# A fused RWKV-6 attention and multiplicative FFN kernel: GpSimd's data arithmetic moved to other engines, k by DMA transpose from unit 7 on, a new order of work

## The chip, the cores and the metric

The kernel runs on one core of a Trainium2 chip. A core has engines that run their own instruction queues in order: TensorE (PE in the profile, its weight loads PEld), VectorE (DVE), ScalarE (ACT), GpSimd (POOL) and SyncE (SP, which only issues DMAs here). They wait for each other by semaphores. The metric is the device time of one execution in microseconds (us), lower is better. Before the change it is 173.02 us, the median of 3 runs (172.81 to 173.9).

## The reference, cut to what matters

```python
# r, k, v, w: [4 batches, 8 heads, 768 steps, 48], u: [8, 48]
state = np.zeros((B, H, D, D))
for t in range(S):
    cur = np.einsum('bhd,bhe->bhde', u[None] * kt, vt)
    y[:, :, t] = np.einsum('bhd,bhde->bhe', rt, state + cur)
    state = wt[:, :, :, None] * state + np.einsum('bhd,bhe->bhde', kt, vt)
x = y.transpose(0, 2, 1, 3).reshape(B * S, H * D)      # [3072, 384]
out = ((x @ w1) * (x @ w2)) @ w3 @ w_out               # d_ff 1024
```

All inputs and the output are float32 in memory.

## The kernel before, in words

Time is cut into 6 chunks of 128 steps. A **unit** is one chunk of two batches (units 0 and 1 are one batch each), 13 units in all, unit t at `UNITS[t]`. Within a chunk the recurrence is written as masked matmuls; between chunks a state of 48 x 48 per head is carried.

For unit t the steps are, by their names in the program (a name is followed by the unit, and by the batch or group):

- loads: `win`, `kin`, `rin`, `vin`. k, r and v are cast to bf16 on the way, which is done on GpSimd's DMA queue; w stays float32.
- decay: `ln` (ScalarE, log of w), `cs` (TensorE, running sum over time by a triangular matrix), `pc`, `ne`, `e`, `iw` (ScalarE, exponentials of it).
- scaled operands: `KRk` (VectorE, k times a decay), `rw` and `KRr` (VectorE, r times decays). Units 0 to 2 (`RAW`) do r in transposed form with `csT` and `et` instead.
- transposes: `trr` and `trk` on TensorE into PSUM with `trre` and `trke` copying to SBUF, or `dtr` and `dtk` as DMA transposes on SP's queue. Before, `dtr` and `dtk` serve units 9 to 12.
- the u term: `rk` (r times k), `ruk` (times u), `dg` (sum over a head), `dv` (v times that sum).
- scores: `m` (TensorE), then either `msk` (VectorE, product with the mask straight from PSUM) or, for the pairs in `POOL_MASK`, `mcp` (ScalarE, PSUM to SBUF) and `maff` (GpSimd, an affine select in place).
- output: `y` (TensorE: scores times v plus r times state), `yb` (VectorE, adds dv; for units in `Y_PE` TensorE adds dv with an identity, `yd`, and `yb` is a plain copy), then a transpose into xT: `yt` and `xT`, or two DMA transposes `dty`, one for each batch (units 8 to 12).
- state: `kv` (TensorE), `T` (VectorE, sum with the old state), `S` (times the chunk's decay), `Sb` (bf16 copy).

The FFN folds w3 and w_out into one matrix w34 at the start: `wt` (transposes on TensorE), `w3Te`, `wm` (64 matmuls), `w34e`. Then **block** t does for four groups of 256 hidden units (two groups of 512 for units 0 and 1) `a` and `b` (TensorE, x times w1 and w2), `asb` (copy of a to SBUF), `abT` (VectorE, the product), and for each batch `o` (TensorE, times w34), `osb` (copy) and `st` (store). `a` and `b` need xT, `o` needs all of w34.

The order of everything is written out by hand. `ORDER` lists every step once with the engine or queue that issues it (`abT_3_1@DVE`), and each engine runs its own steps in that order. `PLACES` gives each step's buffer or PSUM banks. `warm7@15` is 15 filler matmuls into bank 7, which keep TensorE busy while it has nothing else. The lists are data only: the code in `unit`, `block`, `w34_block` and `loads` registers one function for each name, and the last loop of the kernel calls them in the order given.

Lines of the profile that matter here: L389 the unit loads, L400 to L415 the weight loads, L486 and L491 `cs`, L575 `trr`, L590 `trk`, L579 and L594 the copies behind them, L569 and L584 `dtr` and `dtk`, L598 `rk`, L618 `ruk`, L624 `dg`, L633 `dv`, L647 `m`, L653 `mcp`, L661 `maff`, L666 `msk`, L700 `yd`, L706 and L709 `yb`, L718 `dty`, L728 `yt`, L732 `xT`, L752 `T`, L757 to L761 `S`, L786 `a` and `b`, L792 `asb`, L796 `abT`, L802 `o`, L808 `osb`, L813 `st`, L373 the fillers.

Of the kernel before, what the change touches and what calls it, by code (L numbers as in the profile page):

```python
# [862 lines left out]
```

## Time and profile before

| | before |
|---|---|
| median of 3 runs | 173.02 us |
| span of the profiled execution | 172.3 us |
| busy: TensorE / VectorE / ScalarE / GpSimd | 160.0 / 133.2 / 94.1 / 97.8 us |
| fillers on TensorE (L373) | 27, 9.9 us |
| GpSimd: dv (9), maff (8), S (8) | 12.0, 8.8, 7.7 us |
| GpSimd's wait before maff, for mcp | 29.0 us |
| median time of a two-batch k load from issue to landing | 9.3 us |

How to read the profile: busy is the time in which an engine has an instruction running, with overlaps counted once; an instruction's own duration is a little more than its distance to the next one of a row, since instructions overlap at their ends. A busy TensorE is not a TensorE at its peak, since the ends of matmuls are modelled. Spans on GpSimd are rough. The part of the kernel that bounds it is read from the stretches in which an engine stands still, and from the chain of work that ended last. Issuing a load costs GpSimd 1.13 to 1.16 us each, which counts as its busy time.

### The profile page before, as it was taken

The numbers are of one execution on the slowest core, as the hardware profiler recorded it, in microseconds if no ns is written. First come the engines' busy times: TensorE is split into PE (matmuls) and PEld (weight loads), VectorE is DVE, ScalarE is ACT, GpSimd is POOL, SyncE is SP. The second block draws the span as 40 slices with busy tenths as digits, with TensorE's granted clock in tenths as the row PEclk, the third lists the DMA queues.
The fourth block names the chain that finished last, engine by engine and source line by source line (L and its number), as shares of the span: only waits on it lengthen the run. The fifth ranks groups of instructions, "written<-read, shape, count | busy, mean of one in ns | idle before, by whom it ended". The sixth has DMA issues, their size and how long they took to land.

```text
span 172.3 us, 4685 instructions
## 1 busy us (share of the span) xinstructions
PE 160.0 (93%) x1956; PEld 119.6 (69%) x1956; DVE 133.2 (77%) x222; ACT 94.1 (55%) x161; POOL 97.8 (57%) x99
## 2 busy tenths in 40 slices
PE   5889999989999999599999999989989899999990
PEld 2364658558897789357778878667767687886750
DVE  4022798989889999969999899997988745856660
ACT  2125387867568699449888769855661430110301
POOL 7975968699988879694599972040057520000000
PEclk9999999999999999969999999999999999999999
DMA  4999999999999999999999999547879803400333
GB/s 70 159 200 171 235 178 189 177 184 163 170 196 175 163 161 197 175 160 205 71 61 234 119 68 157 111 125 158 166 154 111 142 12 83 137 0 4 137 137 139
DMA packets 98663, 24.36 MB, mean 141 GB/s; under 512 B 88833, under 2 KB 97026, under 8 KB 98642
## 3 DMA queue, kind: packets, MB, share of 16 engines
q0 software_dynamic: 81536, 16.06, 107.9%
q1 hardware_dynamic: 17106, 8.00, 18.9%
q8 instruction: 15, 0.25, 0.6%
q14 instruction: 6, 0.05, 0.1%
HBM read 27.79 MB, written 4.72 MB: 189 GB/s over the span
## 4 chain that ended last, share of the span: by engine, by line
PE 54%; DMA 17%; DVE 13%; ACT 5%; POOL 3%; issue 2%; SPq 2%; ACTq 0%; DVEq 0%; POOLq 0%
PE banks L786 25%; PE banks L802 13%; DMA xT<-yb 6%; DMA wo_bf<-in_moe_w_out_dram 6%; DMA win<-in_w_dram 5%; PE banks L437 4%; DVE abT L796 4%; DVE ruk L618 3%; PE banks L647 2%; PE banks L690 2%; PE banks L486 1%; SPq L813 1%; PE banks L744 1%; POOL w_bf L415 1%; DVE rk L598 1%
## 5 line engine op out<-in xcount | busy, mean ns | idle before, releaser
L786 PE MATMUL banks<-xT,w_bf 128*128 128x256 bf16 (+1 forms) x624 | 70.3, 265 | 1.9 <-DMA xT<-yb 1.9
L786 PEld LDWEIGHTS <-w_bf 128*128 128x128 bf16 x624 | 55.9, 98 | 10.4 <-issue 1.9
L796 DVE TENSOR_TENSOR abT<-a_sb,banks 128x512 bf16<-128x512 f32 x48 | 32.1, 680 | 8.8 <-PE banks L786 8.1
L792 ACT COPY a_sb<-banks 128x512 f32<-128x512 f32 x38 | 22.2, 593 | 27.6 <-DVE abT L796 16.0
L802 PE MATMUL banks<-w,abT 128*128 128x384 bf16 x192 | 36.0, 334 | 0.0
L661 POOL TENSOR_SCALAR_AFFINE_SELECT Mbf<-Mbf 128x1024 bf16<-128x1024 bf16 x8 | 8.8, 1096 | 31.5 <-ACT Mbf L653 29.0
L802 PEld LDWEIGHTS <-abT 128*128 128x128 bf16 x192 | 18.3, 99 | 11.2 <-issue 1.0
L666 DVE TENSOR_TENSOR Mbf<-banks,mask 128x1024 bf16<-128x1024 f32 x16 | 19.3, 1216 | 2.3 <-PE banks L647 2.1
L808 ACT COPY osb<-banks 128x384 f32<-128x384 f32 x18 | 8.7, 491 | 20.7 <-PE banks L802 12.4
L389 POOL DMA_DIRECT2D kin<-in_k_dram x13 | 14.6, 1128 | 1.9 <-DVE KK L505 1.2
L389 POOL DMA_DIRECT2D vin<-in_v_dram x13 | 14.8, 1136 | 0.8 <-DMA wo_bf<-in_moe_w_out_dram 0.7
L389 POOL DMA_DIRECT2D rin<-in_r_dram x13 | 14.7, 1135 | 0.2 <-issue 0.2
L389 POOL DMA_DIRECT2D win<-in_w_dram x12 | 13.9, 1156 | 1.5 <-DMA wo_bf<-in_moe_w_out_dram 1.2
L633 POOL TENSOR_TENSOR dv<-vin,dg 128x768 bf16<-128x768 bf16 (+1 forms) x9 | 12.0, 1345 | 4.4 <-DMA vin<-in_v_dram 1.6
L470 ACT ACTIVATE lw<-win 128x768 bf16<-128x768 f32 (+1 forms) x13 | 10.4, 806 | 7.1 <-DMA win<-in_w_dram 7.1
L709 DVE TENSOR_TENSOR yb<-banks,dv 128x768 bf16<-128x768 f32 x10 | 9.5, 954 | 3.8 <-issue 1.7
L437 PE MATMUL banks<-wo_bf,w3T 128*128 128x384 bf16 x64 | 11.9, 326 | 0.3 <-DMA wo_bf<-in_moe_w_out_dram 0.3
L373 PE MATMUL banks<-zeros 128*128 128x512 bf16 x27 | 9.9, 508 | 1.8 <-DVE zeros L288 1.8
L624 DVE TENSOR_REDUCE dg<-ruk 128x16 f32<-128x768 bf16 (+1 forms) x13 | 11.4, 879 | 0.1
L500 ACT ACTIVATE NEt<-banks 128x768 bf16<-128x768 f32 (+1 forms) x13 | 10.0, 778 | 1.5 <-PE banks L491 0.9
L647 PE MATMUL banks<-RT,KT 64*128 64x128 bf16 x192 | 8.7, 218 | 1.9 <-DVE RT L579 1.4
L653 ACT CAST Mbf<-banks 128x1024 bf16<-128x1024 f32 x8 | 8.2, 1020 | 3.9 <-PE banks L647 2.7
(86 smaller groups left out, 232.7 us busy)
## 6 DMA issues: line engine op xcount, KB each, us to landing
out_dram<-osb SPq DMA_DIRECT2D x24, 192.0 KB, 2.1
win<-in_w_dram POOLq DMA_DIRECT2D x11, 384.0 KB, 8.9
kin<-in_k_dram POOLq DMA_DIRECT2D x11, 192.0 KB, 9.3
rin<-in_r_dram POOLq DMA_DIRECT2D x11, 192.0 KB, 9.4
vin<-in_v_dram POOLq DMA_DIRECT2D x11, 192.0 KB, 7.6
w_bf<-in_moe_w_dram POOLq DMA_DIRECT2D x8, 192.0 KB, 7.1
w_bf<-in_moe_w_dram POOLq DMA_DIRECT2D x4, 256.0 KB, 8.5
w_bf<-in_moe_w_dram POOLq DMA_DIRECT2D x2, 512.0 KB, 8.8
```

Of the source, the lines that this page charges most:

```text
L389: QUEUE[eng].dma_start(dst, src)
L437: nc.tensor.matmul(one(f"wm{fi}")[:, :DM], lhsT=x[:, gi, :], rhs=wo_bf[:, gi, :], start=(gi == 0), stop=(gi == FI - 1))
L470: nc.scalar.activation(LW[:, :, :D], ww, Act.Ln)
L500: nc.scalar.activation(dst, cs_view(), Act.Exp, scale=-1.0)
L624: nc.vector.reduce_sum(dgs, ruks, axis=AX.X)
L633: e.tensor_mul(dvs, vv, dgs[:, :, None].to_broadcast([C, bh, D]))
L647: nc.tensor.matmul(o[:, e, q, :], lhsT=KTs[a:a + PAD, b * HP + q, :], rhs=RTs[a:a + PAD, b * HP + q, :], start=True, stop=True)
L666: nc.vector.tensor_mul(Mbf[m].rearrange("s j q t -> s (j q) t"), mview().rearrange("s j q t -> s (j q) t"), mask[:, None, :].to_broadcast( ...
L786: nc.tensor.matmul(o[:, f, :], lhsT=wt[:, di, fi * P:(fi + 1) * P], rhs=x[:, di, :T], start=(di == 0), stop=(di == DI - 1))
L792: copier(eng)(sa, one(f"a{t}_{g}"))
L796: nc.vector.tensor_mul(ab[:, g * per:(g + 1) * per, :T], sa.rearrange("p (f t) -> p f t", t=T), one(f"b{t}_{g}").rearrange("p (f t) -> p f ...
L802: nc.tensor.matmul(one(f"o{t}_{b}")[:, :DM], lhsT=ab[:, fi, b * C:(b + 1) * C], rhs=w34[:, fi, :], start=(fi == 0), stop=(fi == FI - 1))
```

## The change

Five things change. The code that computes stays the same but for a few places; most of the difference is in the two lists.

1. **GpSimd does no arithmetic on data.** All 13 `dv` and all 11 `S` run on VectorE (before 4 and 3). `maff` runs on VectorE as a product with the mask, in place in SBUF. GpSimd keeps the loads, LT, I128 and the mask, and two affine selects on a small u matrix. `POOL_MASK` now names 12 pairs instead of 8, so 12 of the 24 masks go by `mcp` and `maff`, and 12 by `msk` (before 16).
2. **k by DMA transpose from unit 7** (the eighth): `dtk_7` and `dtk_8` are new, and `dty_7_0`, `dty_7_1` too. `trr` stays on TensorE for units 7 and 8.
3. **The last tile in halves:** o_12_0, osb_12_0 and st_12_0 become two parts of 192 columns.
4. Unit 11's `dg` is computed on TensorE (`PE_DIAG`): a DMA transpose of rk (`dtd_11`), six matmuls of 8 columns (`d_11`), a copy (`dcp_11`), with a small matrix of u made by `ucol`, `ublk` and `ublk2`. `yd` serves units 5 and 7 instead of 0, 1 and 2.
5. **A new order, new banks and buffers.** Among others win_0 goes to GpSimd's queue, eight of the stores to ScalarE's, the first block matmul is a_0_0 instead of a_2_0, and some `asb`, `osb`, `trre`, `trke`, `w3Te`, `yb`, `xT` and `Sb` change between ScalarE and VectorE.

Steps by engine, before and after, where the number changes:

| step | engine | before | after |
|---|---|---|---|
| dv | VectorE / GpSimd | 4 / 9 | 13 / 0 |
| S | VectorE / GpSimd | 3 / 8 | 11 / 0 |
| maff | VectorE / GpSimd | 0 / 8 | 12 / 0 |
| msk | VectorE | 16 | 12 |
| mcp | ScalarE | 8 | 12 |
| asb | ScalarE / VectorE | 38 / 10 | 42 / 6 |
| osb | ScalarE / VectorE | 18 / 6 | 20 / 5 |
| trre | ScalarE / VectorE | 3 / 3 | 6 / 0 |
| st | SP / ScalarE | 24 / 0 | 17 / 8 |
| trk, yt, yd | TensorE | 9, 8, 3 | 7, 7, 2 |
| DMA transposes | SP | 18 | 23 |
| fillers | TensorE | 27 | 29 |

The core of the diff; of the two lists only the pieces that the prediction speaks of (the start up to the first block matmul, the stretch around unit 7, the end):

```diff
 RAW = {0, 1, 2}
 DMA_R = {9, 10, 11, 12}
-DMA_K = {9, 10, 11, 12}
-DMA_Y = {8, 9, 10, 11, 12}
-PE_DIAG = set()
-POOL_MASK = {(5, 1), (6, 1), (7, 1), (8, 1), (9, 1), (10, 1), (11, 1), (12, 1)}
-Y_PE = {0, 1, 2}
+DMA_K = {7, 8, 9, 10, 11, 12}
+DMA_Y = {7, 8, 9, 10, 11, 12}
+PE_DIAG = {11}
+HALF = {(12, 0)}
+POOL_MASK = {(0, 0), (3, 0), (5, 1), (6, 0), (6, 1), (8, 0), (8, 1), (9, 1), (10, 0), (10, 1), (11, 1), (12, 1)}
+Y_PE = {5, 7}
...
 ORDER = """
-urow@SP table@ACT padr_0@DVE padrr1@DVE padkk0@DVE win_0@SP padet0@DVE w3_1@POOL padkk1@DVE zeros@DVE ones2@DVE
-win_1@POOL padlw1@DVE padrr0@DVE padlw0@DVE ones@DVE padet1@DVE padr_1@DVE w3_5@POOL w3_3@POOL wo_0@POOL rin_1@POOL
-wo_1@POOL LT@POOL rin_0@POOL kin_1@POOL ln_1@ACT ln_0@ACT kin_0@POOL warm7@15 cs_0@PE I128@POOL warm7@3 wt_2_0@PE
-wt_6_0@PE wt_7_0@PE w3_0@POOL csT_0@PE wt_6_1@PE wt_7_1@PE w3Te_6_1@DVE wt_2_1@PE w3Te_7_1@DVE wt_3_0@PE w3_2@POOL
-w3Te_6_0@ACT csT_1@PE w3Te_2_1@DVE wt_3_1@PE w3Te_7_0@ACT w3Te_2_0@DVE cs_1@PE w3Te_3_1@DVE et_0@ACT w3Te_3_0@DVE
-et_1@ACT warm1@3 wm_3_0@PE win_2@POOL ne_1@ACT ne_0@ACT wm_6_0@PE ucast@ACT w3_4@POOL wm_7_0@PE warm1@1 wm_7_1@PE
-vin_0@POOL wm_2_0@PE w34e_7@DVE vin_1@POOL wm_2_1@PE KRk_1@DVE kin_2@POOL umm@PE KRk_0@DVE trr_1@PE trr_0@PE ucp@ACT
-KRr_1@DVE wm_6_1@PE pc_0@ACT w34e_2@ACT rk_1@DVE rin_2@POOL ruk_1@DVE wt_0_0@PE trk_0@PE rk_0@DVE wt_1_0@PE ruk_0@DVE
-trk_1@PE w34e_6@DVE wm_3_1@PE win_3@POOL trke_1@ACT KRr_0@DVE wt_1_1@PE trke_0@ACT wt_0_1@PE w3Te_1_0@DVE m_1_0@PE
-mask@POOL w3Te_0_0@ACT dg_0@DVE vin_2@POOL wm_1_0@PE w3Te_0_1@ACT msk_1_0@DVE wm_0_0@PE ln_2@ACT rin_3@POOL wm_0_1@PE
-dg_1@DVE w3Te_1_1@ACT pc_1@ACT m_0_0@PE w34e_3@ACT w34e_0@DVE cs_2@PE msk_0_0@DVE wm_1_1@PE ne_2@ACT wt_5_0@PE
-wt_5_1@PE kv_0@PE w3Te_5_0@ACT dv_0@POOL wt_4_0@PE S_0@DVE wt_4_1@PE w3Te_5_1@ACT w34e_1@DVE kv_1@PE csT_2@PE
-dv_1@POOL Sb_0@DVE S_1@DVE y_0@PE yd_0@PE pc_2@ACT w3Te_4_0@DVE y_1@PE win_4@POOL yd_1@PE yb_0@ACT padr_2@DVE
-KRk_2@DVE wm_5_0@PE et_2@ACT w3Te_4_1@DVE trk_2@PE kin_3@POOL trke_2@ACT rk_2@DVE trr_2@PE wm_4_0@PE ruk_2@DVE
-w1_0@POOL KRr_2@DVE wm_5_1@PE w1_1@POOL dg_2@DVE m_2_1@PE w34e_5@ACT wm_4_1@PE yb_1@ACT msk_2_1@DVE ln_3@ACT m_2_0@PE
-kv_2@PE dv_2@POOL iw_3@ACT msk_2_0@DVE cs_3@PE yt_0@PE w34e_4@ACT ne_3@ACT xT_0@DVE warm0@1 y_2@PE w2_0@POOL S_2@DVE
-yd_2@PE yt_1@PE w2_1@POOL yb_2@DVE ln_4@ACT vin_3@POOL rw_3@DVE warm1@3 yt_2@PE e_3@ACT cs_4@PE w1_2@POOL KRk_3@DVE
-xT_2@ACT KRr_3@DVE warm1@1 trk_3@PE w1_3@POOL pc_3@ACT xT_1@DVE trr_3@PE trke_3@ACT rk_3@DVE rin_4@POOL a_2_0@PE
-trre_3@DVE a_0_0@PE ruk_3@DVE asb_2_0@ACT w2_3@POOL ne_4@ACT dg_3@DVE m_3_1@PE a_2_1@PE w2_2@POOL Sb_1@ACT msk_3_1@DVE
...
-o_12_0@PE osb_12_1@DVE st_10_1@SP st_12_1@SP osb_12_0@ACT st_12_0@SP
+rin_0@POOL padet0@DVE padet1@DVE zeros@DVE ones2@DVE padkk1@DVE urow@SP ucast@ACT ones@DVE warm0@2 umm@PE table@ACT
+kin_0@POOL ucp@ACT padr_1@DVE padlw0@DVE win_0@POOL I128@POOL ln_0@ACT padr_0@DVE padkk0@DVE padlw1@DVE rk_0@DVE
+win_1@POOL w3_1@POOL LT@POOL warm0@4 trr_0@PE warm0@4 cs_0@PE ln_1@ACT csT_1@PE vin_1@POOL w3_3@POOL kin_1@POOL
+rin_1@POOL w3_5@POOL wo_0@POOL vin_0@POOL wo_1@POOL win_2@POOL cs_1@PE csT_0@PE wt_3_0@PE ne_1@ACT et_0@ACT KRr_0@DVE
+w3Te_3_0@DVE warm0@7 wt_2_1@PE ucol@SP ne_0@ACT KRk_1@DVE KRk_0@DVE warm1@4 trk_0@PE wt_2_0@PE kv_1@PE wt_3_1@PE
+rk_1@DVE padrr0@DVE ublk@DVE ruk_1@DVE w3Te_3_1@DVE mask@POOL w3_4@POOL kin_2@POOL rin_2@POOL w3_0@POOL win_3@POOL
+w3_2@POOL w3Te_2_0@ACT et_1@ACT pc_0@ACT w3Te_2_1@DVE padr_2@DVE pc_1@ACT S_1@DVE warm3@6 wt_6_1@PE wt_7_1@PE trr_1@PE
+trke_0@DVE m_0_0@PE trk_1@PE dg_1@DVE w3Te_7_1@ACT wt_7_0@PE ruk_0@DVE mcp_0_0@ACT trke_1@DVE dv_1@DVE KRr_1@DVE
+w3Te_7_0@DVE wm_2_0@PE kv_0@PE S_0@DVE dg_0@DVE wt_6_0@PE Sb_0@ACT w3Te_6_1@ACT m_1_0@PE wm_3_0@PE msk_1_0@DVE
+w3Te_6_0@DVE wm_2_1@PE wm_3_1@PE w34e_3@ACT ln_2@ACT wm_6_0@PE wm_6_1@PE w34e_6@DVE w34e_2@DVE y_1@PE cs_2@PE warm0@2
+wm_7_0@PE ne_2@ACT padrr1@DVE yb_1@DVE dv_0@DVE vin_2@POOL w1_1@POOL w2_1@POOL w1_0@POOL rin_3@POOL wt_5_1@PE
+wt_4_0@PE csT_2@PE wt_5_0@PE yt_1@PE w3Te_5_0@DVE xT_1@DVE KRk_2@DVE wm_7_1@PE w34e_7@DVE w3Te_5_1@DVE et_2@ACT
+w3Te_4_0@ACT pc_2@ACT maff_0_0@DVE rk_2@DVE ruk_2@DVE kin_3@POOL wm_5_0@PE trk_2@PE trr_2@PE wt_4_1@PE w3Te_4_1@ACT
+KRr_2@DVE wt_0_0@PE trke_2@ACT wm_5_1@PE wt_1_0@PE y_0@PE wm_4_0@PE wm_4_1@PE w3Te_1_0@ACT ln_3@ACT w34e_4@ACT
+yb_0@DVE w3Te_0_0@DVE w34e_5@DVE dg_2@DVE w2_0@POOL w2_3@POOL w1_3@POOL w1_2@POOL win_4@POOL w2_2@POOL m_2_1@PE
+yt_0@PE msk_2_1@DVE wt_1_1@PE wt_0_1@PE m_2_0@PE msk_2_0@DVE wm_0_0@PE cs_3@PE w3Te_0_1@ACT e_3@ACT w3Te_1_1@ACT
+Sb_1@ACT dv_2@DVE wm_0_1@PE y_2@PE yb_2@DVE wm_1_0@PE wm_1_1@PE yt_2@PE iw_3@ACT ne_3@ACT pc_3@ACT xT_2@ACT xT_0@DVE
+kv_2@PE S_2@DVE rw_3@DVE KRr_3@DVE a_0_0@PE a_2_0@PE w34e_0@ACT asb_0_0@ACT vin_3@POOL asb_2_0@DVE KRk_3@DVE rk_3@DVE
...
+KRr_8@DVE KRk_8@DVE dtk_7@SP trre_7@ACT abT_5_3@DVE dtk_8@SP st_3_0@ACT st_2_1@ACT b_6_3@PE trr_8@PE kv_7@PE rk_8@DVE
+a_6_3@PE kv_8@PE abT_5_2@DVE kin_11@POOL T_7@DVE T_8@DVE abT_5_1@DVE a_6_0@PE trre_8@ACT asb_6_3@ACT a_6_1@PE ln_9@ACT
+asb_6_1@ACT asb_6_0@ACT abT_6_3@DVE b_6_1@PE b_6_0@PE abT_6_1@DVE iw_9@ACT asb_5_0@ACT b_5_0@PE m_7_1@PE vin_12@POOL
+ublk2@POOL vin_10@POOL rin_9@POOL win_12@POOL abT_6_0@DVE m_8_1@PE a_6_2@PE msk_7_1@DVE asb_6_2@DVE abT_5_0@DVE
+dv_7@DVE mcp_8_1@ACT Sb_5@ACT o_4_0@PE osb_4_0@ACT cs_9@PE pc_9@ACT ln_10@ACT ne_9@ACT iw_10@ACT e_9@ACT m_7_0@PE
+b_6_2@PE o_4_1@PE msk_7_0@DVE abT_6_2@DVE maff_8_1@DVE S_7@DVE KRk_9@DVE m_8_0@PE o_5_0@PE y_7@PE cs_10@PE mcp_8_0@ACT
+ruk_8@DVE kin_12@POOL rin_10@POOL rin_11@POOL vin_11@POOL yd_7@PE maff_8_0@DVE o_6_1@PE yb_7@ACT Sb_7@ACT e_10@ACT
+ne_10@ACT pc_10@ACT osb_4_1@ACT o_6_0@PE kv_9@PE dty_7_0@SP dty_7_1@SP dg_8@DVE rw_9@DVE rk_9@DVE dv_8@DVE KRr_9@DVE
+T_9@DVE rw_10@DVE y_8@PE yb_8@DVE ruk_9@DVE ln_11@ACT st_3_1@ACT ln_12@ACT iw_11@ACT st_2_0@SP osb_6_0@ACT o_5_1@PE
+dtr_9@SP KRk_10@DVE rk_10@DVE dty_8_1@SP dtk_9@SP a_7_1@PE a_7_0@PE asb_7_0@ACT a_7_2@PE a_7_3@PE b_7_1@PE asb_7_2@ACT
...
+asb_12_3@DVE abT_12_2@DVE st_10_0@SP asb_12_1@ACT asb_12_0@ACT abT_12_1@DVE abT_12_0@DVE o_11_1@PE b_12_3@PE o_11_0@PE
+abT_12_3@DVE o_12_1@PE osb_11_1@DVE osb_11_0@ACT st_11_0@SP st_9_1@SP st_11_1@ACT o_12_0_1@PE osb_12_1@DVE o_12_0_0@PE
+st_12_1@SP osb_12_0_1@DVE st_12_0_1@SP osb_12_0_0@ACT st_12_0_0@SP
 """
...
     Et = many(N_ET, [C, BH, D], BF, "Et")
     NEt = many(N_NE, [C, BH, D], BF, "NEt")
     ETt = many(N_ETT, [P, NB * HP, C + 2], BF, "ETt")
-    RTr = many(N_RTR, [P, NB * HP, C], BF, "RTr")
+    RTr = many(N_RTR if RAW & DMA_R else 0, [P, NB * HP, C], BF, "RTr")
     KK = many(N_KK, [C, BH, PAD], BF, "KK")
     RR = many(N_RR, [C, BH, PAD], BF, "RR")
-    rkT = many(N_RKT, [P, NB * DI, C], BF, "rkT")
+    rkT = many(N_RKT if PE_DIAG else 0, [P, NB * DI, C], BF, "rkT")
     KT = many(N_KT, [P, NB * HP, C], BF, "KT")
     RT = many(N_RT, [P, NB * HP, C], BF, "RT")
     Mbf = many(N_M, [C, 2, HP, C], BF, "Mbf")
...
             def _(eng):
                 if c == 0:
                     nc.vector.tensor_mul(Sp, kvv(), PCb)
-                elif c < NC - 2:
-                    nc.gpsimd.tensor_mul(Sp, Tp, PCb)
                 else:
-                    nc.gpsimd.tensor_mul(Bp, Tp, PCb)
+                    e = nc.gpsimd if eng == "POOL" else nc.vector
+                    e.tensor_mul(Sp if c < NC - 2 else Bp, Tp, PCb)
 
             if c < NC - 2:
                 @op(f"Sb_{t}")
...
                 nc.vector.tensor_mul(ab[:, g * per:(g + 1) * per, :T], sa.rearrange("p (f t) -> p f t", t=T),
                                      one(f"b{t}_{g}").rearrange("p (f t) -> p f t", t=T))
         for b in range(nb):
-            @op(f"o_{t}_{b}")
-            def _(eng, b=b):
-                for fi in range(FI):
-                    nc.tensor.matmul(one(f"o{t}_{b}")[:, :DM], lhsT=ab[:, fi, b * C:(b + 1) * C], rhs=w34[:, fi, :],
-                                     start=(fi == 0), stop=(fi == FI - 1))
             so = osb[bank[f"so{t}_{b}"]]
-
-            @op(f"osb_{t}_{b}")
-            def _(eng, b=b, so=so):
-                copier(eng)(so, one(f"o{t}_{b}")[:, :DM])
             row = (b0 + b) * S + c * C
-
-            @op(f"st_{t}_{b}")
-            def _(eng, row=row, so=so):
-                QUEUE[eng].dma_start(out[row:row + C, :], so)
+            parts = [("", slice(0, DM))]
+            if (t, b) in HALF:
+                parts = [(f"_{h}", slice(h * DM // 2, (h + 1) * DM // 2)) for h in range(2)]
+            for tag, cols in parts:
+                def ov(tag=tag, cols=cols, b=b):
+                    return one(f"o{t}_{b}{tag}")[:, :cols.stop - cols.start]
+
+                @op(f"o_{t}_{b}{tag}")
+                def _(eng, b=b, cols=cols, ov=ov):
+                    for fi in range(FI):
+                        nc.tensor.matmul(ov(), lhsT=ab[:, fi, b * C:(b + 1) * C], rhs=w34[:, fi, cols],
+                                         start=(fi == 0), stop=(fi == FI - 1))
+
+                @op(f"osb_{t}_{b}{tag}")
+                def _(eng, so=so, cols=cols, ov=ov):
+                    copier(eng)(so[:, cols], ov())
+
+                @op(f"st_{t}_{b}{tag}")
+                def _(eng, row=row, so=so, cols=cols):
+                    QUEUE[eng].dma_start(out[row:row + C, cols], so[:, cols])
 
     for fi in range(FI):
         w34_block(fi)
```

161 lines of the change are left out of this document (76 added, 85 removed).

## The prediction

> **What bounds the kernel now.** I read the page's busy row first, then busy time by stretch, then the chain that ended last, and then the groups and the timeline around the one place where TensorE stands still.
>
> ```profile
> PE 160.0 (93%) x1956; PEld 119.6 (69%) x1956; DVE 133.2 (77%) x222; ACT 94.1 (55%) x161; POOL 97.8 (57%) x99
> ```
>
> ```profile
> 0.00:39.40 39.40, 35.16 (x358) 21.36 (x359) 23.45 (x60) 20.88 (x39) 31.79 (x41) 1.00 1.55 174
> 39.40:145.30 105.90, 102.00 (x1426) 81.18 (x1424) 93.96 (x138) 69.73 (x116) 66.03 (x59) 0.98 1.43 143
> 145.30:168.20 22.90, 22.85 (x178) 17.03 (x175) 15.76 (x25) 3.00 (x6) 0.00 (x0) 1.00 0.25 82
> 168.20:172.30 4.10, 0.00 (x0) 0.00 (x0) 0.00 (x0) 0.48 (x1) 0.00 (x0) 0.91 0.35 126
> ```
>
> Columns: length, busy time of PE, PEld, DVE, ACT and POOL, granted clock, DMA share, GB/s. I cut at the first block matmul (39.4), at the end of y_12 (145.3) and at the last matmul (168.2). TensorE is the bound: from the first block on it is idle for 3.9 + 0.05 us out of 128.8. So the change can win in four places only: the 39.4 us before the blocks, those 3.9 us with the slow clock that goes with them, TensorE's own work, and the last 4.1 us. VectorE is the second bound: 93.96 + 15.76 = 109.7 us of the same 128.8.
>
> **The change part by part.** *Start.* The chain shows why the first block begins at 39.4:
>
> ```profile
> 27.89 8.74 DMA win<-in_w_dram
> ...
> 37.61 0.48 PE banks L486 x2
> ...
> 38.51 0.45 PE banks L590 x8
> 39.00 0.61 PE banks L575 x8
> ```
>
> win_4 lands at 36.6; cs_4 (L486), trk_3 (L590) and trr_3 (L575) stand ahead of a_2_0 in TensorE's order. In the new order a_0_0 comes first and all three stand behind it; a_0_0 needs xT_0 and weight quarters w1_0 and w1_1. I count what GpSimd's queue has to bring, by tile sizes (a two-batch w 384 KB, a two-batch k, r or v 192 KB, half of each for units 0 and 1; w3 2,048 KB, w_out 768 KB, a quarter of w1 or w2 192 KB). Before, up to win_4: w 1,536 + r 576 + k 384 + v 384 + w3 2,048 + w_out 768 = 5,696 KB. After, up to w1_0: w 1,152 + r 384 + k 384 + v 384 + 2,048 + 768 + three quarters 576 = 5,696 KB. The same amount, so I put a_0_0 at 36.7, a gain of 2.7. Some of that is lent: cs_4 0.48, trk_3 0.45 and trr_3 0.45, about 1.4 us of TensorE, now lie behind the first block. Term **-1.3**. Bounds: no gain in time, so +1.4, up to a first block at 34, so -4.0. win_0 leaves SP's queue for third place in GpSimd's, behind rin_0 and kin_0, so cs_0 comes later; what covers that is that TensorE then waits for w3 and w_out anyway; without that cover it costs up to the 2.7. More and differently placed fillers (27 to 29) fall into these waits and cost nothing for the same reason. u_col's load, u_blk's copy and two GpSimd masks on 3x8 elements are needed only by d_11, 80 us later: nothing.
>
> *TensorE's work after the first block.*
>
> ```profile
> 73.14 2.67 PE banks L802 x8
> ...
> 78.17 1.33 PE banks L786 x12
> 79.50 1.30 PE banks L802 x8
> 80.81 0.34 PE banks L728 x6
> ```
>
> Gone: trk_7 and trk_8 (2 x 0.45, L590 above) and yt_7 (0.34). New: yd_5 and yd_7, four matmuls of 384 columns (0.24 each by L486's 0.48 for two, about 0.9) and d_11, six of 8 columns (at most 0.3, as L728's six). yd_0 to yd_2 go from the start, where they were waited over. Two halves of o_12_0 have 16 matmuls of 192 columns for eight of 384: 1.30 together. Sum -0.9 - 0.3 + 0.9 + 0.2 = -0.1; with yd at 0.16 each, if they stream as L802's 384 columns do, -0.4. I take the latter: **-0.4**, between -0.7 and +0.5.
>
> *The stall that GpSimd's arithmetic causes.* The longest wait in the middle begins on VectorE. Groups of its instructions between 63 and 76 us (busy, mean ns of one):
>
> ```profile
> L618 DVE TENSOR_TENSOR ruk<-rk,u_bc 128x768 bf16<-128x768 bf16 x1 | 3.1, 3080 | 0.0
> L796 DVE TENSOR_TENSOR abT<-a_sb,banks 128x512 bf16<-128x512 f32 x3 | 2.0, 671 | 0.0
> L624 DVE TENSOR_REDUCE dg<-ruk 128x16 f32<-128x768 bf16 x2 | 1.9, 935 | 0.0
> L666 DVE TENSOR_TENSOR Mbf<-banks,mask 128x1024 bf16<-128x1024 f32 x1 | 1.2, 1209 | 0.0
> L598 DVE TENSOR_TENSOR rk<-rin,kin 128x768 bf16<-128x768 bf16 x1 | 1.2, 1180 | 0.0
> L505 DVE TENSOR_TENSOR KK<-kin,NEt 128x768 bf16<-128x768 bf16 x2 | 1.1, 545 | 0.0
> L564 DVE TENSOR_TENSOR RR<-rw,Et 128x768 bf16<-128x768 bf16 x2 | 1.0, 550 | 0.0
> L579 DVE COPY RT<-banks 128x1024 bf16<-128x1024 bf16 x1 | 0.7, 677 | 0.0
> L594 DVE COPY KT<-banks 128x1024 bf16<-128x1024 bf16 x1 | 0.7, 676 | 0.0
> L752 DVE TENSOR_TENSOR Tst<-banks,Sst 128x384 f32<-128x384 f32 x1 | 0.5, 540 | 0.0
> ```
>
> Instructions of one size and type take 0.55 (L505, L564), but this ruk took 3.08 and this rk 1.18: 3.2 us too long. GpSimd's timeline (start, length) has dv_5 (L633) beside ruk:
>
> ```profile
> 60.36 2.28 POOL L389 DMA_DIRECT2D rin<-in_r_dram  x2
> ...
> 67.29 1.16 POOL L389 DMA_DIRECT2D win<-in_w_dram  x1
> 68.46 1.50 POOL L633 TENSOR_TENSOR dv<-vin,dg 128x768 bf16<-128x768 bf16 x1
> ```
>
> ```profile
> 66.50:72.20 5.70, 3.78 (x46) 3.11 (x45) 5.70 (x7) 3.71 (x6) 4.56 (x4) 1.00 2.34 186
> 72.20:75.90 3.70, 3.68 (x33) 2.10 (x33) 3.02 (x4) 0.92 (x3) 3.35 (x4) 0.55 1.80 171
> ```
>
> TensorE was idle for 1.92 us (5.70 - 3.78), then had clock 0.55, at which eight L802 matmuls took 2.67 instead of 1.30. Together 1.92 + 1.37 = 3.3. All 25 such instructions on GpSimd (nine dv, eight maff, eight S) go, so **-3.3**; between -3.3 and 0. The next late thing there is m_5's operand chain through VectorE, below. The Trainium skill, "TensorE: Matmul & The Clock Gate", Part 1, has the array fall to half clock after about 3.4 us of idleness; with 1.92 us, in pieces, it would not have fallen, the term would be -1.9 and the sum 1.4 more. The row with 0.55 decides for the fall.
>
> *What VectorE takes over.*
>
> ```profile
> L633 DVE TENSOR_TENSOR dv<-vin,dg 128x768 bf16<-128x768 bf16 x4 | 4.7, 1186 | 0.0
> ```
>
> Added: dv, seven of full and two of half size, at most 8 x 1.19 = 9.5; S, 8 x 0.54 (L752, same size, two f32 operands) = 4.3; maff as a product with the mask in SBUF, 12 of 128x1024 bf16: no row has it; between 0.68 (L579, same size and type) and 1.21 (L666, from PSUM), nearer to the first because 768 bf16 elements from SBUF take 0.55: 8.2. Together 22.0. Removed: four msk 4.8, four a_sb copies (0.67 as L796) 2.7, three trre 2.0, ruk_11 and dg_11 1.5, three single copies of about 0.55, 1.6: 12.6. Less 3.2 of the stall: net +6.2, of which some 1.5 (dv_0 to dv_2, maff_0_0) falls before the blocks. VectorE then has 109.7 + 4.7 = 114.4 us in about 125: 91% instead of 85%. That hides it on average; behind a late VectorE instruction queue the next unit's KRr, trr and m, and TensorE waits for those. Each stretch of that sort is short, so I charge **+0.7** (0 to +6).
>
> ScalarE gets four mcp, four a_sb copies, three trre and eight store issues more, about 12 us on 94: its 55% leave room, and I charge nothing; what hides it is TensorE's 93%. GpSimd's queue only issues loads now: nothing in it waits for arithmetic any more, so loads come earlier, bounded by free buffers. No load was waited for after 39.4, so this earns nothing.
>
> *More DMA transposes.* SP's queue gets dtk_7, dtk_8, dty_7_0, dty_7_1 and dtd_11 more, and loses seven stores to ScalarE's.
>
> ```profile
> kin<-in_k_dram POOLq DMA_DIRECT2D x11, 192.0 KB, 9.3
> ...
> xT<-yb SPq DMA_TRANSPOSE x10, 2.3
> RT<-RR SPq DMA_TRANSPOSE x4, 3.6
> KT<-KK SPq DMA_TRANSPOSE x4, 3.0
> ```
>
> Cover for dtk_7 before m_7_1: seven block groups (L786 x12 is two, 0.66 each), trr_8, kv_7 and kv_8, about 5.8 us against 3.0 to land: nothing. Cover for dty_7 before a_7_1: o_6_1, o_6_0, o_5_1 (1.30 each), yd_7, kv_9 and y_8, about 5.6; against it yb_7 on ScalarE (0.8), two issues and 2.3 to 3.6 until landing, 5.5 to 7: **+1.0**, between 0 and +2. Dtk_8 and the stores behind these on SP's queue are not waited for at once. The other dty waits stay as they are.
>
> *End.* The last half copies 192 columns instead of 384: of the last row's 0.48 at best half goes: **-0.2** (0 to -0.5).
>
> Sum: -1.3 - 0.4 - 3.3 + 0.7 + 1.0 - 0.2 = -3.5. The profiled execution has a span of 172.3, 0.7 below the median of the runs, 173.0. So span 168.8, predicted time 169.5 us, 2% less.
>
> **The rivals.** *The start pays and the transposes are hidden.* First block at 35 and no wait at a_7_1, VectorE's part hidden: -1.7 - 1.0 - 0.7, so 166.1. For it: GpSimd reaches w1_0 without a dv in between. Against: the same 5,696 KB.
>
> *The stall stays.* If descriptor writing for loads, not dv_5, held ruk up, the loads are still there, and the time is 169.5 + 3.3 = 172.8. For it: the win issue at 67.29 began beside ruk, and dv_5 only later.
>
> ```profile
> 61.92 1.02 DVE L556 TENSOR_TENSOR rw<-rin,iw 128x768 bf16<-128x768 bf16 x2
> ```
>
> Against: these two took 1.02 together, undisturbed, inside the two issues of 60.36. The Trainium skill, "SBUF — State Buffer", section "Who interferes with whom", says that of a VectorE instruction with two SBUF inputs and a GpSimd one that reads SBUF the first to start keeps the port and the other waits. By that ruk, first by this trace, would not have waited for dv_5; GpSimd's starts are rough, so this leaves the rival alive. VectorE becoming the bound ends at the same place: twelve maff at 1.21 add 6.4 us, VectorE has 97%, and half of it shows, 172.7.
>
> *Slower: transposes among the loads.* dtk_7, dtk_8 and dty_7 run while loads are still in flight. If they land as loads do, in 9.3, m_7_1 waits 1.3 + 9.3 - 5.8 = 4.8 and a_7_1 0.8 + 2.5 + 9.3 - 5.6 = 7.0, against 1.0 charged: 169.5 + 10.8 = 180.3. Slower than before by over 1% takes 5.3 us more than forecast, from a landing of about 6.3 on. Against: the slowest kind of transpose landed in 3.6 (median).
>
> **How the numbers follow.** Forecast (167.5 to 171.2) 0.46; the good start 0.22; the stall stays or VectorE bounds 0.18; slow transposes 0.08; other waits from the new order, worse than charged by over 5 us, 0.06. A measurement of this kernel can tell about 1% from no change, so faster is below 171.3 and slower above 174.7: 0.46 + 0.22 = 0.68, 0.18, and 0.08 + 0.06 = 0.14. The range leaves out a tenth at either end: 165.0 (start and all waits together, a little beyond 166.1) to 174.5 (172.8 and some of the wait that slow transposes cost).
>
> **What would show it.** Right: no VectorE product of 768 elements over 0.7 us; no clock below 0.9 after the first block; first block matmul at 36 to 37.5; maff near 0.68; VectorE near 139 us busy, GpSimd near 70. Wrong: TensorE idle over 5 us between the first block and the end, with waits for L579, L594 or L666; transposes over 5 us until landing; a first block after 39.

## The result: 0.8% slower, and the profile after

| | before | after |
|---|---|---|
| median of 18 runs each | 173.45 us | 174.67 us |
| span of the profiled execution | 172.3 us | 173.5 us |
| first block matmul | 39.4 us | 39.9 us (predicted 36.7) |
| from there to the end | 132.9 us | 133.6 us (predicted 132.1) |

The ratio after to before is 1.0078, 95% interval 1.0048 to 1.0107: a loss of about 1.3 us where 3.5 us of gain were predicted. (The ratio leaves out executions more than 1.5% above the fastest of their kernel, so it is not quite the ratio of the two medians.) 174.67 lies just above the range. Against the predicted span of 168.8 there are 4.7 us of the profiled execution to explain: 3.2 before the first block and 1.5 behind it.

The profile's busy row of the new kernel, and its busy time by stretch (columns as before: length, PE, PEld, DVE, ACT, POOL, clock, DMA share, GB/s):

```profile
PE 160.5 (92%) x1948; PEld 117.8 (68%) x1948; DVE 134.7 (78%) x237; ACT 104.0 (60%) x174; POOL 71.1 (41%) x77
```

```profile
0.00:22.60 22.60, 16.51 (x126) 7.84 (x127) 10.68 (x38) 9.58 (x17) 18.61 (x27) 1.00 1.23 157
22.60:39.90 17.30, 16.91 (x203) 11.55 (x203) 12.81 (x23) 10.45 (x19) 11.81 (x13) 1.00 1.88 186
39.90:169.00 129.10, 127.03 (x1622) 98.43 (x1620) 110.92 (x176) 83.60 (x139) 40.71 (x38) 0.99 1.29 140
169.00:173.50 4.50, 0.00 (x0) 0.00 (x0) 0.33 (x1) 0.32 (x1) 0.00 (x0) 0.73 0.27 89
```

GpSimd went from 97.8 to 71.1 us and VectorE from 133.2 only to 134.7. From the first block to the last matmul TensorE is idle for 2.07 us of 129.1 (before 3.95 of 128.8).

TensorE's waits, from the view of waits (who waits for whom, total, times, longest), and the fillers among the groups:

```profile
PE banks L788 <- DMA xT<-yb: 2.0, 1, 2.0
PE banks L426 <- DMA w_bf<-in_moe_w_dram: 1.8, 3, 0.8
PE banks L376 <- DVE zeros L291: 1.3, 1, 1.3
PE banks L440 <- DMA wo_bf<-in_moe_w_out_dram: 1.2, 1, 1.2
```

```profile
L376 PE MATMUL banks<-zeros 128*128 128x512 bf16 x29 | 9.6, 465 | 1.3 <-DVE zeros L291 1.3
```

After the first block one wait is left, 2.0 us for xT: it is a_7_1 (L788 now) waiting for unit 7's new DMA transpose. TensorE's timeline (start, length, what ended the idle time) and the chain of waits at that place:

```profile
108.59 1.46 PE L813 MATMUL banks<-w,abT 128*128 128x384 bf16 x8
112.00 6.41 PE L788 MATMUL banks<-xT,w_bf 128*128 128x256 bf16 x42 [1.96 <-DMA xT<-yb]
118.35 0.40 PE L650 MATMUL banks<-RT,KT 64*128 64x128 bf16 x8
```

```profile
105.00 0.36 ACT yb L709
...
107.70 0.29 SPq L721
107.99 0.04 issue
108.03 3.83 DMA xT<-yb
```

SP's timeline and the DMA issues (median us to landing) show what the transposes cost:

```profile
89.84 2.88 SPq L587 DMA_TRANSPOSE KT<-KK  x2
105.83 3.46 SPq L721 DMA_TRANSPOSE xT<-yb  x2
```

```profile
xT<-yb SPq DMA_TRANSPOSE x12, 3.6
KT<-KK SPq DMA_TRANSPOSE x6, 3.5
RT<-RR SPq DMA_TRANSPOSE x4, 3.2
```

yb_7 is ready at 105.8, two issues hold SP for 3.46 us, and the second transpose lands at 111.9, 3.83 after its issue. The block that waited then ran its 42 matmuls in 6.41 us, at a lower clock, as the seventh number by stretch shows:

```profile
108.00:114.00 6.00, 4.04 (x54) 2.83 (x49) 5.56 (x10) 2.92 (x6) 0.00 (x0) 0.92 1.37 151
114.00:120.00 6.00, 6.00 (x61) 4.47 (x60) 2.74 (x5) 3.93 (x8) 0.00 (x0) 0.80 0.69 160
```

VectorE's groups by shape (busy, mean ns of one) show the contention gone and the new products at the predicted lengths:

```profile
L636 DVE TENSOR_TENSOR dv<-vin,dg 128x768 bf16<-128x768 bf16 x11 | 10.4, 948 | 0.0
L662 DVE TENSOR_TENSOR Mbf<-Mbf,mask 128x1024 bf16<-128x1024 bf16 x12 | 8.1, 682 | 0.1
L601 DVE TENSOR_TENSOR rk<-rin,kin 128x768 bf16<-128x768 bf16 x11 | 6.0, 550 | 0.0
L508 DVE TENSOR_TENSOR KK<-kin,NEt 128x768 bf16<-128x768 bf16 x11 | 6.0, 550 | 0.0
L621 DVE TENSOR_TENSOR ruk<-rk,u_bc 128x768 bf16<-128x768 bf16 x10 | 5.5, 551 | 0.1
L763 DVE TENSOR_TENSOR Sst<-Tst,pc 128x384 f32<-128x384 f32 x6 | 3.3, 549 | 0.0
```

### The profile page after: what moved, and what is told of

It reads as the page before. It is cut to its first block, busy times and chain, and to the rows that moved or that the text cites. A ratio compares the mean times of both kernels' runs of the same rounds, so it can differ in the third digit from the quotient of the medians.

```text
span 173.5 us, 4680 instructions
## 1 busy us (share of the span) xinstructions
PE 160.5 (92%) x1948; PEld 117.8 (68%) x1948; DVE 134.7 (78%) x237; ACT 104.0 (60%) x174; POOL 71.1 (41%) x77
## 4 chain that ended last, share of the span: by engine, by line
PE 74%; DMA 8%; POOL 6%; ACT 4%; DVE 3%; issue 2%; SPq 0%; POOLq 0%; ACTq 0%
PE banks L788 38%; PE banks L813 16%; DMA wo_bf<-in_moe_w_out_dram 6%; PE banks L650 4%; PE banks L440 3%; PE banks L693 3%; DMA xT<-yb 2%; PE banks L489 2%; PE banks L687 2%; PE banks L578 2%; PE banks L747 1%; POOL w_bf L418 1%; PE banks L593 1%; POOL kin L392 1%; POOL rin L392 1%
## 5 line engine op out<-in xcount | busy, mean ns | idle before, releaser
L788 PE MATMUL banks<-xT,w_bf 128*128 128x256 bf16 (+1 forms) x624 | 72.1, 268 | 2.0 <-DMA xT<-yb 2.0
L788 PEld LDWEIGHTS <-w_bf 128*128 128x128 bf16 x624 | 55.6, 99 | 11.0 <-DMA xT<-yb 2.3
L794 ACT COPY a_sb<-banks 128x512 f32<-128x512 f32 x42 | 24.5, 594 | 21.3 <-PE banks L788 17.9
L813 PE MATMUL banks<-w,abT 128*128 128x384 bf16 (+1 forms) x200 | 34.5, 320 | 0.0
L656 ACT CAST Mbf<-banks 128x1024 bf16<-128x1024 f32 x12 | 12.2, 1015 | 7.3 <-PE banks L650 6.0
L818 ACT COPY osb<-banks 128x384 f32<-128x384 f32 (+1 forms) x20 | 9.4, 481 | 10.8 <-PE banks L813 7.8
L669 DVE TENSOR_TENSOR Mbf<-banks,mask 128x1024 bf16<-128x1024 f32 x12 | 14.4, 1217 | 0.7 <-PE banks L650 0.5
L636 DVE TENSOR_TENSOR dv<-vin,dg 128x768 bf16<-128x768 bf16 (+1 forms) x13 | 11.5, 888 | 0.0
L712 DVE TENSOR_TENSOR yb<-banks,dv 128x768 bf16<-128x768 f32 (+1 forms) x11 | 9.6, 877 | 1.4 <-ACT a_sb L794 1.1
L440 PEld LDWEIGHTS <-w3T 128*128 128x128 bf16 x64 | 5.8, 97 | 5.9 <-issue 2.4
L601 DVE TENSOR_TENSOR rk<-rin,kin 128x768 bf16<-128x768 bf16 (+1 forms) x13 | 6.8, 526 | 3.6 <-DMA kin<-in_k_dram 3.6
```

Source lines behind the costliest of these rows:

```text
L440: nc.tensor.matmul(one(f"wm{fi}")[:, :DM], lhsT=x[:, gi, :], rhs=wo_bf[:, gi, :], start=(gi == 0), stop=(gi == FI - 1))
L636: e.tensor_mul(dvs, vv, dgs[:, :, None].to_broadcast([C, bh, D]))
L656: copier(eng)(Mbf[m], mview())
L669: nc.vector.tensor_mul(Mbf[m].rearrange("s j q t -> s (j q) t"), mview().rearrange("s j q t -> s (j q) t"), mask[:, None, :].to_broadcast( ...
L788: nc.tensor.matmul(o[:, f, :], lhsT=wt[:, di, fi * P:(fi + 1) * P], rhs=x[:, di, :T], start=(di == 0), stop=(di == DI - 1))
L794: copier(eng)(sa, one(f"a{t}_{g}"))
```

## The experiments

All were timed beside the kernel before; ratios are to it, and the new kernel itself has 1.0078. Most diffs are in steps of the lists, and `...` marks what is left out.

**Unit 7's y back on TensorE** (y7_pe): only the dty_7 part of the change is undone.

```diff
-DMA_Y = {7, 8, 9, 10, 11, 12}
+DMA_Y = {8, 9, 10, 11, 12}
-o_6_0@PE kv_9@PE dty_7_0@SP dty_7_1@SP
+o_6_0@PE kv_9@PE yt_7@PE xT_7@ACT
```

> The changed kernel with one part undone: unit 7's y goes to xT by TensorE (yt_7, xT_7 on ScalarE) instead of two DMA transposes. Theory A (the wait at a_7_1 is the DMA transposes' landing, and the slow clock follows from it): the 1.96 us wait and the 1.8 us of slow clock behind it go, 0.34 us of transposes come, so 3.4 us less than the changed kernel, about 171.2, faster than before. Theory B (ScalarE and VectorE are what is late there, the wait only shows first at a_7_1): the wait moves to the next step, and the time changes by less than 1 us.

171.67 us, ratio 0.9923 (0.9887 to 0.9959). TensorE's timeline at a_7_1 has no wait any more and the 42 matmuls run at full clock:

```profile
109.32 1.46 PE L813 MATMUL banks<-w,abT 128*128 128x384 bf16 x8
110.62 4.75 PE L788 MATMUL banks<-xT,w_bf 128*128 128x256 bf16 x42
```

So this one transpose cost about 2.7 us (1.0078 - 0.9923, of 173.45; with the two intervals 1.9 to 3.5), and without it the change is a gain.

**Fillers into that gap** (fill_gap): the wait stays, TensorE stays warm.

```diff
+warm2@9
 a_7_1@PE
```

> The changed kernel with nine filler matmuls (1.9 us) ahead of a_7_1, which fill the wait without shortening it. If the clock falls because TensorE stands still there: clock 1.00 behind the wait, the 42 block matmuls take 4.6 instead of 6.4 us, 1.8 us less, about 172.9. If the clock falls for another reason: no change, 174.7.

174.07 us, ratio 1.0079 (1.0043 to 1.0116): nothing came back, though in its profile the fillers stand in the wait and the 42 matmuls run at full clock:

```profile
110.66 4.75 PE L788 MATMUL banks<-xT,w_bf 128*128 128x256 bf16 x42
```

The lower clock of the new kernel's profiled execution is therefore not what costs on the median; the wait is. The next kernel shows the same.

**The last tile whole again** (whole_tile).

```diff
-HALF = {(12, 0)}
+HALF = set()
-o_12_0_1@PE osb_12_1@DVE o_12_0_0@PE st_12_1@SP osb_12_0_1@DVE st_12_0_1@SP osb_12_0_0@ACT st_12_0_0@SP
+osb_12_1@DVE o_12_0@PE st_12_1@SP osb_12_0@ACT st_12_0@SP
```

> The changed kernel with the last tile in one piece (one o, one copy, one store). Theory: the second half's store is issued 0.43 us behind the first on the same queue and lands no sooner for being half, so the whole tile ends 0.3 to 0.4 us earlier, minus about 0.15 us for the longer copy: 0.2 to 0.3 us less than the changed kernel. Rival (halves pay as meant): 0.2 us more.

173.92 us, ratio 1.0066 (1.0033 to 1.0099): the halves earn nothing that can be told from zero. Its timeline has nearly the same wait at a_7_1, here with no fall of the clock. (S, named in the row, only ended at about the same moment: in y7_pe a_7_1 begins at 110.62 and that S at 111.85.)

```profile
110.67 4.75 PE L788 MATMUL banks<-xT,w_bf 128*128 128x256 bf16 x42 [1.85 <-DVE Sst L763]
```

**GpSimd's arithmetic to VectorE in the old order** (before_dve): the kernel before with all dv, maff and S of GpSimd on VectorE, at the same places of the list.

```diff
-dv_5@POOL maff_5_1@POOL S_4@POOL
+dv_5@DVE maff_5_1@DVE S_4@DVE
...
```

> The kernel before with one part of the change alone: its 25 instructions of data arithmetic on GpSimd (nine dv, eight maff, eight S) run on VectorE, in the same places of the order. Theory A (GpSimd's arithmetic holds VectorE up): no product of 768 elements over 0.7 us, the stall at 70 us with its slow clock goes, 3 us less than before less what the added work costs, 170.5 to 172. Theory B (descriptor writing holds it up): ruk near 3 us stays, and the time is 173 or, with VectorE 14 us fuller, more, up to 176.

177.60 us, ratio 1.0259 (1.0211 to 1.0306). The stretch from the first block to 145 in its busy time by stretch:

```profile
39.74:145.00 105.26, 98.31 (x1375) 78.43 (x1373) 100.85 (x158) 70.27 (x116) 41.32 (x37) 1.00 1.44 140
```

TensorE is idle for 7.0 us there instead of 3.9: VectorE has 100.9 us instead of 94.0, and the steps of the old order wait for it. The contention goes, and more than its worth is paid. This kernel does not have what else the change takes off VectorE (12.6 us by the prediction's count), so it does not price the change's own load on VectorE.

**Only the colliding product moved, in the old order** (before_dv5).

```diff
-dv_5@POOL
 msk_5_0@DVE
+dv_5@DVE
```

> The kernel before with one instruction moved: unit 5's dv, the one beside which ruk took 3.08 us, goes from GpSimd to VectorE, behind unit 5's second mask product; all else stays. Theory A (the term of the prediction): ruk takes 0.55, TensorE's 1.92 us of waits at 68 to 72 shrink to under 0.5 and the eight matmuls at low clock are gone, so 2 to 3 us less, a ratio of 0.982 to 0.989. Rival B (a fall of the clock is not what costs, as with the fillers put into the gap, and VectorE has to do the 0.95 us that GpSimd did): the wait goes, but only 0.5 to 1.5 us come back, ratio 0.991 to 0.997. Rival C (next to it waits another product, so that nothing comes back): 0.997 to 1.004.

170.96 us, ratio 0.9933 (0.9890 to 0.9975). VectorE's timeline has the ruk that had taken 3.08 us:

```profile
66.78 0.55 DVE L619 TENSOR_TENSOR ruk<-rk,u_bc 128x768 bf16<-128x768 bf16 x1
```

GpSimd's timeline still has the issue of a win load beside this ruk:

```profile
66.77 1.16 POOL L390 DMA_DIRECT2D win<-in_w_dram  x1
```

So dv_5 was what held ruk up, and not the load's issue. What comes back is 1.2 us (0.4 to 1.9) and not 3.3. One moved step in the kernel before does as much as the best version of the whole change, within the intervals.

**GpSimd's arithmetic back, in the new order** (after_pool): the steps that ran on GpSimd before run there again, at their new places (maff as an affine select).

```diff
-dv_5@DVE maff_5_1@DVE S_5@DVE
+dv_5@POOL maff_5_1@POOL S_5@POOL
...
```

> The changed kernel with 24 of the arithmetic instructions put back on GpSimd, at their places in the new order: the nine dv, eight S and seven maff that before had there. Theory A (GpSimd's arithmetic holds up VectorE's products and the loads queued behind it, which outweighs the 14 us of VectorE work): some products over 1 us, time above the changed kernel by 1 to 3 us, 176 to 178. Theory B (a fuller VectorE costs more than it saves, as in the kernel before with the arithmetic on VectorE): below the changed kernel by 1 to 3 us, 172 to 173.5.

184.68 us, ratio 1.0598 (1.0518 to 1.0677), 9 us above the new kernel. VectorE's groups and GpSimd's waits say why:

```profile
L602 DVE TENSOR_TENSOR rk<-rin,kin 128x768 bf16<-128x768 bf16 x11 | 9.9, 896 | 0.0
...
L509 DVE TENSOR_TENSOR KK<-kin,NEt 128x768 bf16<-128x768 bf16 x11 | 9.3, 844 | 0.0
```

```profile
POOL Mbf L665 <- ACT Mbf L657: 20.5, 4, 8.4
POOL Mbf L665 <- PE banks L748: 14.0, 1, 14.0
```

rk and KRk are stretched from 0.55 to 0.90 and 0.84 on average, and the loads queue behind a GpSimd that waits 34.5 us in these two rows before its masks. On TensorE the longest of the waits from this is again the one of a_7_1:

```profile
119.15 7.61 PE L789 MATMUL banks<-xT,w_bf 128*128 128x256 bf16 x42 [3.84 <-DMA xT<-yb]
```

So part of the 9 us comes through unit 7's transpose. This order was not made for arithmetic on GpSimd, as the old one was not made without: moving the arithmetic to VectorE costs 2.6% there and earns 5% here, with unit 7's y by DMA.

**The old start in the new kernel** (start_before): every engine's steps up to the first block matmul in the order of before, without GpSimd's arithmetic, and the mask of unit 0 by msk. The first loads of the two orders:

```diff
-rin_0@POOL kin_0@POOL win_0@POOL win_1@POOL w3_1@POOL vin_1@POOL w3_3@POOL kin_1@POOL rin_1@POOL w3_5@POOL wo_0@POOL
-vin_0@POOL wo_1@POOL
+win_0@SP w3_1@POOL win_1@POOL w3_5@POOL w3_3@POOL wo_0@POOL rin_1@POOL wo_1@POOL rin_0@POOL kin_1@POOL kin_0@POOL
...
```

> The changed kernel with the order of before up to the first block matmul (loads, TensorE's folding of w3 and w_out, units 0 to 2; GpSimd still without arithmetic on data, unit 0's mask by msk). Theory A (the new order puts the loads of units 0 and 1 ahead of w3 and w_out, w_out's second half lands at 22.6 instead of 16.5, and the folding waits): w_out by 17 us, first block matmul at 37 to 38 instead of 39.9, 2 to 3 us less than the changed kernel, about 172. Theory B (the start is bounded by all bytes up to w1_0, 5,696 KB in both): first block at 39.5 or later, no gain, 174.7.

175.81 us, ratio 1.0146 (1.0090 to 1.0201). w_out is issued earlier there, and yet the first block comes at 40.08, now behind VectorE and ScalarE:

```profile
36.98 0.58 PE L693 MATMUL banks<-vin,Mbf 128*128 128x48 bf16 x16 [1.13 <-DVE Mbf L669]
...
40.08 2.11 PE L788 MATMUL banks<-xT,w_bf 128*128 128x128 bf16 x26 [0.75 <-ACT pc L550]
```

**y by TensorE and the tile whole** (y7_whole), and the same **with the old start** (y7_whole_start); the edits are those above, together.

> The changed kernel with unit 7's y by TensorE and the last tile whole. If both add up: 3.0 and 0.3 to 0.7 less than the changed kernel, 171.0 to 171.4. If the store was not in the way: 171.7, as with unit 7 alone.

> The same with the start of before as well. Theory A on the start: another 2 to 3 us, 168 to 169.5, faster than both kernels. Theory B: no less than without it, 171 to 171.7.

171.52 us, ratio 0.9899 (0.9856 to 0.9943), and 172.31 us, ratio 0.9958 (0.9923 to 0.9994). The first is the best variant of the new kernel. It differs from whole_tile in unit 7's y alone, so this pair prices that transpose a second time: 1.0066 - 0.9899, 2.9 us. Its busy time by stretch from the first block to 165:

```profile
38.90:165.00 126.10, 124.62 (x1615) 96.97 (x1612) 110.59 (x174) 84.40 (x140) 40.85 (x38) 1.00 1.29 140
```

TensorE is idle for 1.5 us of 126: what is left lies before the first block and in TensorE's own work.

**w_out earlier** (early_wo), on y7_whole; the loads and TensorE's steps that change:

```diff
-win_1@POOL w3_1@POOL LT@POOL vin_1@POOL w3_3@POOL kin_1@POOL rin_1@POOL w3_5@POOL wo_0@POOL vin_0@POOL wo_1@POOL
+win_1@POOL w3_1@POOL LT@POOL w3_3@POOL wo_0@POOL wo_1@POOL vin_1@POOL kin_1@POOL rin_1@POOL w3_5@POOL vin_0@POOL
-warm3@6 wt_6_1@PE wt_7_1@PE
+wm_2_0@PE wm_3_0@PE wm_2_1@PE wm_3_1@PE wt_6_1@PE wt_7_1@PE
```

> The new kernel with unit 7's y by TensorE and the last tile whole (ratio 0.990 to before so far), and in it the start changed: the two loads of w_out are issued ahead of unit 1's v, k and r (about 7.2 and 8.0 instead of 10.3 and 12.0), and the first four half folds take the place of three fillers, ahead of the transposes of the sixth load of w3. Theory A (the late landing of w_out holds the folding up, as the timeline of the start suggests): the first block matmul comes at 36 to 37.3 instead of 38.9, and the time falls by 1 to 2.5 us, ratio 0.976 to 0.984. Rival B (the loads of units 0 and 1 and VectorE's work on them set the start as much as w_out does): the first folds start at 17 to 18, but the units are late by as much, first block at 38.3 to 39.5, ratio 0.987 to 0.995.

181.16 us, ratio 1.0526 (1.0469 to 1.0583): far worse than either theory. VectorE's and TensorE's timelines:

```profile
17.80 0.63 DVE L508 TENSOR_TENSOR KK<-kin,NEt 128x384 bf16<-128x384 bf16 x2 [5.68 <-DMA kin<-in_k_dram]
```

```profile
18.48 0.40 PE L593 MATMUL banks<-I,KK 128*128 128x128 bf16 x4 [2.10 <-DVE KK L508]
...
47.38 2.48 PE L788 MATMUL banks<-xT,w_bf 128*128 128x128 bf16 x30
```

Unit 1's k, pushed behind w_out, lands at 17.8. VectorE stands still for 5.7 us in front of it, with the copies that the folding needs queued behind. After the wait of 2.10 us TensorE's clock falls (0.50 from 21 to 24 us in the busy time by stretch), and the folds, which were to win by the earlier w_out, run at half speed:

```profile
20.57 5.28 PE L440 MATMUL banks<-wo_bf,w3T 128*128 128x384 bf16 x16 [0.69 <-DVE w3T L434]
```

In the new kernel 16 such matmuls take 2.76 us. The first block slides to 47.4; from there to the end it takes 131.2 us, about as in y7_whole (130.8), so the loss lies ahead of it.

**k of units 7 and 8 on TensorE** (k7_pe), on y7_whole.

```diff
-DMA_K = {7, 8, 9, 10, 11, 12}
+DMA_K = {9, 10, 11, 12}
-dtk_7@SP dtk_8@SP b_6_3@PE kv_7@PE a_6_3@PE
+b_6_3@PE trk_7@PE trke_7@ACT kv_7@PE a_6_3@PE trk_8@PE trke_8@ACT
```

> The new kernel with unit 7's y by TensorE and the last tile whole, and k of units 7 and 8 transposed by TensorE again (two times eight matmuls, about 1.0 us, and two copies on ScalarE, about 1.6 us), instead of by the two DMA transposes that land in 4.6 to 5.1 us and are not waited for there. Theory A (a transpose by DMA that is covered saves TensorE's time): 1.0 to 2.0 us more, ratio 0.996 to 1.002. Rival B (TensorE's place for them costs nothing, because waits behind them shrink, or the two transposes held something else up): ratio 0.987 to 0.993, as without the edit.

175.96 us, ratio 1.0241 (1.0172 to 1.0310), 5.9 us above y7_whole, more than theory A's 1 to 2. TensorE's timeline:

```profile
91.21 0.43 PE L747 MATMUL banks<-vin,KK 128*64 128x48 bf16 x16 [0.65 <-ACT KT L597]
...
93.95 0.43 PE L747 MATMUL banks<-vin,KK 128*64 128x48 bf16 x16 [1.10 <-ACT KT L597]
```

All PSUM banks are taken there, so kv_7 and kv_8 get the banks of these transposes and wait 1.75 us for ScalarE's copies. By 112 the kernel is 2.7 us behind y7_whole (where a_7_1 starts at 109.33 instead of 112.04). Another 1.3 us come later, at a DMA transpose of k that lands too late; at the same place y7_whole waits 0.60:

```profile
126.43 0.40 PE L650 MATMUL banks<-RT,KT 64*128 64x128 bf16 x8 [1.90 <-DMA KT<-KK]
```

Together they cover the 3.8 us between the two profiled spans (173.5 and 169.7), but not all of the 5.9 by the ratios. Why that transpose lands later, and how much of the loss is TensorE's and ScalarE's time and how much this choice of banks, stays open.

## Why the prediction was wrong

**Start (predicted -1.3, first block at 36.7): the step that failed, 3.2 of the 4.7 us.** It counted the bytes that GpSimd's queue brings up to w1_0 and took their end for the limit. The load came as forecast. GpSimd's timeline has the issue of w1_0, which the view of this one instruction shows landing 9.2 us after it, at 36.9:

```profile
27.72 0.78 POOL L403 DMA_DIRECT2D w_bf<-in_moe_w_dram  x1 [0.61 <-DMA kin<-in_k_dram]
```

Yet a_0_0 began at 39.86, and no wait for w1 appears among TensorE's. From 22.6 on TensorE is busy for 16.91 of 17.3 us with folding and units, up to kv_2 directly ahead of a_0_0, and that work sets 39.9. The prediction took the step from the landing to the first block to be free; it did not count the work that stands in TensorE's order in front of the block. A stretch that is full on the bounding engine isn't shortened by an earlier load.

A better measure is TensorE's time without use before the first block, idle and fillers together. Before, it is 39.4 - 35.16 = 4.2 idle and 9.9 of fillers, 14.1. After, it is 39.9 - 33.42 = 6.5 and 9.6, 16.1. The waits for w_out (1.2) and w3 (1.8) in the list above are more than that difference. The w_out wait is in one of the six profiled executions that have this start. Their first blocks come between these two, from the timelines of whole_tile and y7_pe:

```profile
38.65 2.46 PE L788 MATMUL banks<-xT,w_bf 128*128 128x128 bf16 x30
```

```profile
40.15 2.48 PE L788 MATMUL banks<-xT,w_bf 128*128 128x128 bf16 x30
```

On average the first block comes at 39.2 in these six, and at 39.2 in the two with the old start (before and before_dv5). The unused time is 15.0 on average against 14.1. So the start gained nothing, and the work that the prediction called lent to the blocks was paid for: it cost about 1 us by unused time, 1.4 by the prediction's own count, which is its upper bound, and not the 2 us of this one execution. What would shorten it is open: start_before and early_wo show that w_out alone is not it, since k of unit 1 or VectorE is late next.

**DMA transpose of unit 7's y (predicted +1.0, between 0 and +2): right place, mis-sized.** The wait of 1.96 is at the prediction's upper bound; by the times the transpose cost more, 2.7 us (y7_pe) and 2.9 (y7_whole against whole_tile). What it cost above the forecast 1.0 covers the 1.5 us behind the first block. From the first block to the end whole_tile's profile has 133.1 us and y7_whole's 130.8, neither with a fall of the clock at a_7_1; besides the wait of 1.85 some tenths come from waits for transposes behind it. Cover was 5.0 us (105.0 to 110.0) instead of 5.6, SP took 3.46 for two issues, and the landing took 3.83, a little above the slowest kind's 3.6. The rival of transposes landing like loads, at 6.3 or more, did not come. dtk_7 and dtk_8 were rightly costed at nothing.

**The stall (predicted -3.3): mechanism right, size wrong.** dv_5 held ruk, though by the trace ruk began first (before_dv5), so the rival of descriptor writing falls. But its removal is worth 1.2 us. The 1.37 of slow clock was read from one execution and charged to all. Of 50 executions of the kernel before that were timed beside the experiments, 27 had a mean granted clock of 0.996 or more and a mean span of 170.4 us; the other 23 had 171.8. So a loss of about the forecast size goes with a lower clock, in about half of them; where in the kernel their clock fell is not shown. In the new kernel the same comparison gives 172.8 and 172.9 us (9 and 8 executions). The clock fell after 1.92 us in pieces in the profile before, and after 1.96 in the new one, but not after 1.85 in whole_tile. The Trainium skill, "TensorE: Matmul & The Clock Gate", Part 1, has the array fall to half clock after at least one idle window of about 3.4 us; by that the term would have been -1.9, nearer to the 1.2. The two falls above came after shorter waits, so here the measurement and the page differ. What decides between a fall and none isn't shown.

**What the forecast left alone, and luck.** "The other dty waits stay as they are" did not hold either. TensorE's waits in the profile before have this row:

```profile
PE banks L786 <- DMA xT<-yb: 1.9, 3, 0.7
```

These three waits, all in the blocks, are not in the new kernel's profile. From the first block to the end the forecast without the transpose is 1.8 us less than before (-0.4 - 3.3 + 0.7 - 0.2 and the 1.4 lent). The profiles of the two variants with y by TensorE have 1.8 (y7_pe) and 2.0 (y7_whole) less. The lump came out, but with a stall that is worth 1.2 by itself and waits for xT that nobody had counted: in part that was luck.

**VectorE (predicted +0.7, 0 to +6).** The lengths were right (maff 0.68, dv 0.95, busy 134.7 against about 139). VectorE's busy time rose by 1.5 us where +6.2 was forecast, and in the new kernel's profile no wait for VectorE is left in the blocks. In the old order, without the relief that the change also brings, stall and load together came to +4.5 us (2.6%), so there the order sets the price; that is not the change's own case, and no run prices the term +0.7 by itself.

**End (predicted -0.2).** In the profile 4.5 us follow the last matmul instead of 4.1; whole_tile and y7_whole show no effect that can be told from zero. TensorE's own work (-0.4) was not tested by itself.

The sum thus becomes: start about +1, transpose +2.7, against them some 2 us or more from the stall, the waits for xT and TensorE's own work. That gives a small loss, as measured, and a gain of 0.8% (0.4 to 1.1, y7_pe) once unit 7's y goes by TensorE. Of these terms only the transpose and dv_5 were isolated by experiments; the start is read from profiles.
